# Packed q/k projections, 1024-column score tiles and one static order for a gated attention and token-MLP kernel on one core

## The chip, the cores and the metric

The kernel runs on one core of one Trainium2 chip. The metric is the device time of one launch in microseconds (us). A kernel's time is the median of its runs; the page and the trace of a kernel come from one profiled run of it.

The engines are named as the profile names them: PE is TensorE (PEld its weight loads, which overlap with matmuls: 216.0 us of them beside 362.7 us of matmuls in a span of 402.6), DVE is VectorE, ACT is ScalarE, POOL is GpSimd, SP is SyncE, which here only starts transfers. Each engine works through its own list of instructions in order, and waits on semaphores for the others.

## The reference, cut to what matters

The input x is 2048 x 640. A is attention with a compressive memory: 32 heads of 20 columns, four segments of 512 rows. Within a segment it is causal softmax attention; from segment 1 on, a linear-attention read of a memory M that sums up earlier segments is mixed in. B normalises x by row and runs an MLP over the token axis. A gate per row mixes A and B.

```python
phi = lambda t: jnp.where(t > 0, t + 1.0, jnp.exp(t))
for s in range(N):                                  # N = 4 segments of L = 512
    qs, ks, vs = q[:, :, s], k[:, :, s], v[:, :, s]
    p = softmax(einsum('bhqd,bhkd->bhqk', qs, ks) * scale + mask)
    a_dot = einsum('bhqk,bhkd->bhqd', p, vs)
    a_mem = (phi(qs) @ M) / (phi(qs) @ z + 1e-06)
    o = g * a_mem + (1.0 - g) * a_dot
    M = M + phi(ks)^T vs ;  z = z + sum(phi(ks))
a = o @ wo                                          # [...]
h = layernorm(x)                                    # over 640 columns
u = gelu(einsum('bsd,sf->bdf', h, w1) + b1)         # 2048 tokens -> 1536
y = einsum('bdf,fs->bds', u, w2) + b2               # 1536 -> 2048 tokens
return gate * a + (1 - gate) * y^T                  # gate = sigmoid(x . gate_w)
```

## The kernel before

The parts that the change touches. A head takes 32 partitions (20 used), so a group of four heads fills 128 and there are 8 groups. The weights of q and k are copied into a zero-padded layout, and every segment needs 8 projections of q and 8 of k, each of 5 matmuls of 512 columns: 320 in all.

```python
# LayerNorm: statistics on DVE, scaling on ACT (3 of 4 tiles) and DVE (1 of 4)
if t % 4 != 3:
    nc.scalar.activation(out=hs[:, t, :], in_=xs[:, t, :], func=ACT.Identity, scale=..., bias=...)
else:
    nc.vector.tensor_scalar(out=hs[:, t, :], in0=xs[:, t, :], scalar1=mv[:, t, 0:1],
                            scalar2=rstd[:, t:t + 1], op0=ALU.subtract, op1=ALU.mult)
# [...] the whole first MLP matmul (w1, gelu) runs here, before any attention
nc.vector.tensor_copy(out=wq_pad[:]...[:, :, :, 1:1 + DH], in_=wq_st[:]...)   # likewise wk_pad

def phi(out_view, x_view, e_view):                  # DVE, ACT, DVE
    nc.vector.tensor_scalar_min(out=e_view, in0=x_view, scalar1=0.0)
    nc.scalar.activation(out=e_view, in_=e_view, func=ACT.Exp)
    nc.vector.scalar_tensor_tensor(out=out_view, in0=x_view, scalar=0.0, in1=e_view, op0=ALU.max, op1=ALU.add)

def st_exp(s, g):                                   # scores, two heads at a time
    for jt in range(TPS):
        Nq = L - jt * P                             # 512, 384, 256, 128 columns
        for hp in range(2):
            psB = pS("psB")
            for rr in range(2):
                nc.tensor.matmul(psB[:, rr, 0:Nq], lhsT=kA[32*r:32*r+32, ...], rhs=qA[32*r:32*r+32, ...],
                                 tile_position=(32 * r, 0))
            nc.scalar.activation(out=pt[...], in_=psB[:, :, 0:Nq], func=ACT.Exp, scale=SCALE)
        nc.gpsimd.affine_select(out=pt[:, :, 0:P], ...)     # causal mask of the diagonal block
# [...]
for s in range(NSEG):                               # the main loop; a scheduler interleaves
    for g in range(G):
        st_exp(s, g); pv_post(*prev)                # scores of this group, PV of the last one
        nat_v(s + 1, g); pg_q(s + 1, g); pg_k(s + 1, g); phi_kT(s + 1, g)   # next segment
        tail_y(...); tail_a(...); tail_b(...)       # second MLP matmul, output projection
```

## Time and profile before

The time before is 403.88 us (median of 3 runs, 403.81 to 411.12; a run more than 1.5% above the fastest, as 411.12 is, counts as slow). The head of the profile page gives busy time by engine, and the span in 40 equal slices with the busy share in tenths (PEclk is the clock that the TensorE throttle granted, in tenths of full speed).

```profile
PE 362.7 (90%) x3705; PEld 216.0 (54%) x3732; DVE 238.6 (59%) x556; ACT 235.0 (58%) x374; POOL 107.2 (27%) x162
PE   3559999959999999998999999999999999999976
POOL 8300000040132223434231323222222233343420
PEclk9759999998999999998999999999999999999998
```

PE is the engine that bounds this kernel: 362.7 of 402.6 us busy, at nine tenths or more in nearly every slice. The next table shows stretches of the span. Its columns are the stretch, its length, then busy us and instructions of PE, PEld, DVE, ACT and POOL, then granted clock, DMA share and GB/s.

```profile
0.00:27.00 27.00, 11.39 (x91) 8.85 (x92) 19.50 (x71) 19.36 (x32) 12.09 (x27) 0.80 0.97 281
27.00:80.00 53.00, 53.00 (x397) 37.84 (x395) 1.30 (x8) 22.35 (x36) 0.08 (x1) 0.97 0.43 118
58.00:104.00 46.00, 41.60 (x332) 25.45 (x333) 16.99 (x32) 14.09 (x24) 6.00 (x5) 0.96 0.16 39
104.00:140.00 36.00, 35.13 (x331) 20.85 (x333) 28.03 (x62) 16.86 (x28) 9.85 (x11) 1.00 0.01 2
88.00:390.00 302.00, 283.84 (x3084) 160.39 (x3110) 206.89 (x458) 192.35 (x305) 90.36 (x132) 0.99 0.08 24
```

From 27 to 80 us PE is busy without one gap, with the first MLP matmul (375 of the 397 instructions; the others are 20 tiny ones of the gate and the flag). From 88 to 390 us it is busy for 283.84 of 302 us, and no other engine is busy for more than 207. Three PE waits (total us, times, longest):

```profile
PE pg_352 L209 <- DVE cmask L270: 6.1, 1, 6.1
PE ptk_1013 L349 <- DVE phikT_990 L316: 2.6, 1, 2.6
PE psB_2444 L444 <- ACT PT_2429 L447: 1.2, 1, 1.2
```

The first lies in start-up (18.5 to 24.5 us): three tiny transposes that compute a flag (see below) wait for what DVE has reduced for them; the profile names cmask, which DVE finished just after it. The second is the longest after start-up. The third is the longest of the waits of a scores tile for the exponential that has its buffer; there are 28 of over 0.15 us, 8.4 us in all. One more number matters for what follows: DVE's own time for the LayerNorm scaling of one 128 x 640 tile, and for one 512-column step of phi (shortest, median and longest in ns, then first and last start).

```profile
L193 DVE TENSOR_SCALAR hs<-xs,mv,rstd x4: 441/443/444, 17.7 to 25.3; 128x640 bf16<-128x640 bf16 x4
L314 DVE TENSOR_SCALAR e_k_1033<-kA_969 x1: 282/282/282, 95.7 to 95.7; 128x512 bf16<-128x512 bf16 x1
```

### The profile page before, as it was taken

The page shows a single profiled execution, that of the slowest core. Times are in us where ns is not written, and L with a number is a line of the kernel's source. Part 1 is how long each engine was busy: PE and PEld are TensorE (multiplying, and loading weights), DVE is VectorE, ACT ScalarE, POOL GpSimd, SP SyncE. Part 2 cuts the span into 40 slices and gives each one's busy share as a digit, 9 for nine tenths or more (in the row PEclk, how much of TensorE's full clock was granted, in tenths as well). Part 3 has the DMA queues.
Part 4 walks back from the last instruction along what each step waited for, and adds up shares of the span by engine and source line. Part 5 has one row for each costly group of instructions (what it writes and reads, how often), then busy time and mean ns, then how long its engine had stood idle before and what let it go on. Part 6 is the DMA issues. An engine that isn't in the chain of part 4 may idle for free.

```text
span 402.6 us, 8992 instructions
## 1 busy us (share of the span) xinstructions
PE 362.7 (90%) x3705; PEld 216.0 (54%) x3732; DVE 238.6 (59%) x556; ACT 235.0 (58%) x374; POOL 107.2 (27%) x162
## 2 busy tenths in 40 slices
PE   3559999959999999998999999999999999999976
PEld 3437777734465555455555455555555554555544
DVE  5850000076886867766777778785766666444444
ACT  2999311233415677965565766655555767788740
POOL 8300000040132223434231323222222233343420
PEclk9759999998999999998999999999999999999998
DMA  6994454000000020020002000200020021000002
GB/s 224 330 314 119 126 154 108 2 0 2 0 2 2 2 79 2 2 80 2 0 18 81 18 2 19 78 18 2 20 80 18 10 74 31 18 2 18 18 21 72
DMA packets 32101, 21.78 MB, mean 54 GB/s; under 512 B 820, under 2 KB 32052, under 8 KB 32052
## 3 DMA queue, kind: packets, MB, share of 16 engines
q1 hardware_dynamic: 31842, 21.11, 18.0%
q8 instruction: 31, 0.51, 0.5%
q14 instruction: 18, 0.15, 0.1%
q10 hardware_dynamic: 210, 0.02, 0.0%
HBM read 18.50 MB, written 2.62 MB: 52 GB/s over the span
## 4 chain that ended last, share of the span: by engine, by line
PE 77%; ACT 12%; DVE 5%; issue 2%; DMA 2%; ACTq 0%; POOL 0%; DVEq 0%; POOLq 0%
DMA beta_bf<-in_A_beta_dram 2%; ACT xT L164 1%; PE pu_369 L234 1%; PE pu_370 L234 1%; DVE qA_968 L320 1%; DVE stats L182 1%; PE pu_772 L234 1%; PE pu_736 L234 1%; PE pu_700 L234 1%; PE pu_664 L234 1%; PE pu_628 L234 1%; PE pu_592 L234 1%; PE pu_554 L234 1%; PE pu_518 L234 1%; PE pu_480 L234 1%
## 5 line engine op out<-in xcount | busy, mean ns | idle before, releaser
L255 DVE TENSOR_SCALAR gt<-gt 128x16 f32<-128x16 f32 x1 | 2.1, 2073 | 40.6 <-ACT gt L254 40.6
L401 PEld LDWEIGHTS <-wk_pad 128*128 128x128 bf16 x160 | 14.8, 99 | 15.5 <-issue 1.4
L374 PEld LDWEIGHTS <-wq_pad 128*128 128x128 bf16 x160 | 12.4, 97 | 11.2 <-issue 2.9
L307 POOL MEMSET vs_970<- 128x128 bf16 x1 | 0.7, 664 | 66.6 <-PE pu_772 L234 66.6
L330 PEld LDWEIGHTS <-xT 128*128 128x128 bf16 x160 | 13.0, 97 | 7.1 <-issue 1.5
L182 DVE BATCH_NORM_STATS2 stats<-xs 128x6 f32<-128x320 bf16 x32 | 13.4, 460 | 4.0 <-DMA xs<-in_A_x_dram 4.0
L444 PEld LDWEIGHTS <-kA_969 32*128 32x128 bf16 x128 | 6.0, 90 | 17.5 <-issue 16.6
L444 PEld LDWEIGHTS <-kA_2515 32*128 32x128 bf16 x128 | 6.1, 90 | 16.4 <-issue 14.9
L444 PEld LDWEIGHTS <-kA_1310 32*128 32x128 bf16 x128 | 5.9, 91 | 15.8 <-issue 14.4
L444 PEld LDWEIGHTS <-kA_3832 32*128 32x128 bf16 x128 | 6.0, 91 | 12.5 <-issue 10.2
L190 ACT ACTIVATE hs<-xs,nmr,rstd 128x640 bf16<-128x640 bf16 x12 | 10.0, 924 | 0.0
L163 PEld LDWEIGHTS <-xs 128*128 128x128 bf16 x80 | 7.3, 126 | 4.5 <-issue 3.8
L234 PEld LDWEIGHTS <-w1c_126 128*128 128x128 bf16 x64 | 7.3, 114 | 3.9
L211 DVE TENSOR_REDUCE gred<-pg_352 1x1 f32<-1x128 f32 x1 | 0.3, 279 | 14.3 <-PE pg_352 L209 14.3
L234 PEld LDWEIGHTS <-w1c_515 128*128 128x128 bf16 x64 | 6.3, 98 | 2.4
L234 PEld LDWEIGHTS <-w1c_132 128*128 128x128 bf16 x64 | 6.3, 98 | 2.4
L234 PEld LDWEIGHTS <-w1c_441 128*128 128x128 bf16 x64 | 6.3, 98 | 2.4
L234 PEld LDWEIGHTS <-w1c_589 128*128 128x128 bf16 x64 | 6.3, 98 | 2.4
L234 PEld LDWEIGHTS <-w1c_130 128*128 128x128 bf16 x64 | 6.3, 98 | 2.4
L209 PE MATMUL pg_352<-ident_f,gstat 128*1 128x128 f32 x3 | 0.9, 306 | 6.1 <-DVE cmask L270 6.1
L234 PE MATMUL pu_369<-hs,w1c_126 128*128 128x320 bf16 x16 | 6.3, 405 | 0.0
L234 PE MATMUL pu_370<-hs,w1c_126 128*128 128x320 bf16 x16 | 6.2, 398 | 0.0
(1883 smaller groups left out, 1389.7 us busy)
## 6 DMA issues: line engine op xcount, KB each, us to landing
xs<-in_A_x_dram SPq DMA_DIRECT2D x4, 640.0 KB, 7.6
w1c_126<-in_B_w_dram SPq DMA_DIRECT2D x1, 1024.0 KB
w1c_130<-in_B_w_dram SPq DMA_DIRECT2D x1, 1024.0 KB
w1c_132<-in_B_w_dram SPq DMA_DIRECT2D x1, 1024.0 KB, 13.1
w1c_441<-in_B_w_dram SPq DMA_DIRECT2D x1, 1024.0 KB, 5.5
w1c_515<-in_B_w_dram SPq DMA_DIRECT2D x1, 1024.0 KB, 5.9
w1c_589<-in_B_w_dram SPq DMA_DIRECT2D x1, 1024.0 KB, 6.2
wq_st<-in_A_wq_dram SPq DMA_DIRECT2D x1, 800.0 KB, 14.0
```

What stands on the lines that cost most here:

```text
L163: nc.tensor.transpose(pt[:, j, :], xs[:, t0 + j, c * P:(c + 1) * P], ident_bf[:])
L164: nc.scalar.copy(out=xT[:, c, t0 * P:(t0 + ST // XC) * P], in_=pt[:].rearrange("p a b -> p (a b)"))
L182: nc.vector.bn_stats(out=stats[:, t, c, :], in_=xs[:, t, c * HALF:(c + 1) * HALF])
L190: nc.scalar.activation(out=hs[:, t, :], in_=xs[:, t, :], func=ACT.Identity, scale=rstd[:, t:t + 1], bias=nmr[:, t:t + 1])
L209: nc.tensor.transpose(pg[:, c, :], gstat[:, c:c + 1], ident_f[:])
L234: nc.tensor.matmul(pu[hh][:, 0:HALF], lhsT=w1c[:, t, f2 * P:(f2 + 1) * P], rhs=hs[:, t, hh * HALF:(hh + 1) * HALF], start=(t == 0), stop=( ...
L255: nc.vector.tensor_scalar(out=gt[:], in0=gt[:], scalar1=0.5, scalar2=0.5, op0=ALU.mult, op1=ALU.add)
L320: nc.vector.tensor_copy(out=out_view, in_=ps_view)
L330: nc.tensor.matmul(pv[hh][:, 0:HALF], lhsT=xT[:, c, t * P:(t + 1) * P], rhs=wv_sb[:, c, hh * HALF:(hh + 1) * HALF], start=(c == 0), stop=( ...
L374: nc.tensor.matmul(pq[:, 0:L], lhsT=wq_pad[:, c, g * P:(g + 1) * P], rhs=xT[:, c, s * L:(s + 1) * L], start=(c == 0), stop=(c == DC - 1))
L401: nc.tensor.matmul(pk2[:, 0:L], lhsT=wk_pad[:, c, g * P:(g + 1) * P], rhs=xT[:, c, s * L:(s + 1) * L], start=(c == 0), stop=(c == DC - 1))
L444: nc.tensor.matmul(psB[:, rr, 0:Nq], lhsT=kA[32 * r:32 * r + 32, g, jt * P:(jt + 1) * P], rhs=qA[32 * r:32 * r + 32, g, jt * P:L], start=T ...
```

## The change

The intent is to take TensorE work away and to fill every hole between scores with other work.

- q and k are projected without padding: 5 chunks of 128 of the 640 columns instead of 8 padded groups, so 200 matmuls of 512 columns instead of 320. In a packed chunk the first 20 rows of each 32 belong to group c, the other 12 carry a piece of groups 5, 6 or 7, which transfers on SP move to their own place.
- Scores go to tiles of 2 x 512 columns that join (g, 3) with (g, 1), and (g, 2) with (g + 1, 2). One visit (a run of scores matmuls between other work on PE) does all four heads: 80 visits instead of 224, and 160 exponentials of 1024 columns.
- LayerNorm scaling, and the add and the min of phi, go to GpSimd. So do two smaller steps that DVE did before: the sum of the two parts of attention and the scaling of M (39 operations). Statistics stay on DVE.
- Everything else on PE (projections, first and second MLP, memory update and read, tail) is a list of items, and a planner written in the kernel takes the next instructions from that list between two scores tiles. The order of each engine is then fixed as written.

```diff
-        nc.vector.tensor_copy(out=wq_pad[:].rearrange(...)[:, :, :, 1:1 + DH], in_=wq_st[:]...)
+    PIECES = [(0, 0, 12, 5, 0), (1, 0, 8, 5, 12), (1, 8, 4, 6, 0), (2, 0, 12, 6, 4),
+              (3, 0, 4, 6, 16), (3, 4, 8, 7, 0), (4, 0, 12, 7, 8)]
+        def ln_apply(ci):                      # [...]
+            nc.gpsimd.tensor_tensor(out=rstd[:, tsl], in0=rstd[:, tsl], in1=mhalf[:], op=ALU.pow)
+            for t in range(tsl.start, tsl.stop):
+                nc.gpsimd.tensor_scalar(out=xs[:, t, :], in0=xs[:, t, :], scalar1=mv[:, t, 0:1],
+                                        scalar2=rstd[:, t:t + 1], op0=ALU.subtract, op1=ALU.mult)
         def phi(out_view, x_view):
-            nc.vector.tensor_scalar_min(out=e_view, in0=x_view, scalar1=0.0)
-            nc.scalar.activation(out=e_view, in_=e_view, func=ACT.Exp)
-            nc.vector.scalar_tensor_tensor(out=out_view, in0=x_view, scalar=0.0, in1=e_view, ...)
+            nc.gpsimd.tensor_scalar(out=out_view, in0=x_view, scalar1=1.0, scalar2=None, op0=ALU.add)
+            nc.scalar.activation(out=e[:], in_=x_view, func=ACT.Exp)
+            # placed 0.8 and 2.2 us of PE work later:
+            nc.gpsimd.tensor_scalar_min(out=e[:], in0=e[:], scalar1=1.0)
+            nc.vector.tensor_tensor(out=out_view, in0=out_view, in1=e[:], op=ALU.max)
+        def mem_update(s, c):                  # transposes, copy, and at once the matmuls that read it
+            for j in range(TPS):
+                nc.tensor.transpose(ptk[:, j, :], pk_[:, j * P:(j + 1) * P], ident_bf[:])
+            nc.vector.tensor_copy(out=nat[:], in_=ptk[:])
+            # [...] matmuls: lhsT=nat[:, j, :]
+        def scores(s, parts):                  # all four heads, up to 2 x 512 columns each
+            tl = [pS("psB"), pS("psB")]
+            for (g, jt) in parts:
+                for r in range(HG):
+                    nc.tensor.matmul(tl[r // 2][:, r % 2, o:o + n], ..., tile_position=(32 * r, 0))
+            return [exp_mask(x, ps_off) for x in tl]
+        # [...] the list of items, in order
+        for t in range(8): add(("ln", t), ...)       # LayerNorm statistics
+        for ci in range(1, 4): add(("xT", ci), ...)  # transposes of x
+        for t in range(8, 16): add(("ln", t), ...)
+        for ci in range(4): call(("lnA", ci), ln_apply, ci)
+        call("flag", flag)
+        # qkv of segment 1; first MLP (merged with qkv of 2); second MLP, tail, qkv of 3
+        for (s, g) in pairs:
+            q0 = scores(s, [(g, 0)]);  filln();  post(*prev)
+            q13 = scores(s, [(g, 3), (g, 1)]);  filln()
+            q2 = scores(s, [(g, 2), (g + 1, 2)]);  filln()
+            # [...] two more visits for g + 1
```

The flag is a number that says whether scores could overflow without a row maximum. Before, it chose between two main parts; now the fast one always runs, and a slow one after it only if the flag says so. With this input it never does.

## The prediction

> What bounds it now. TensorE. The table of stretches gives PE 362.7 of 402.6 us busy: 0 to 27 us is start-up (PE 11.4 busy, loads, transposes, LayerNorm), 27 to 80 is the first MLP matmul alone (PE full, ACT 22 of 53, DVE 1.3), 88 to 390 is attention with everything else (PE 283.8 of 302, ACT 192, DVE 207). So what counts is PE stream time, the start, and whether PE is fed.
>
> PE stream time, from start-to-start distances in the timeline: a 512-column matmul takes 0.216 us (TensorE: Matmul & The Clock Gate, Part 1, states 215.7 ns; the trace agrees), 320 columns 0.136, a 128-column transpose about 0.056, a 21-column PV matmul 0.0255. A visit of scores between full-array matmuls displaces 0.42 us (all four 512s), 0.365 (a 384 pair), 0.31 (256), 0.26 (128), 0.2 of it not streaming. The TensorEngine Tiling page, Key Properties, says that a mode switch drains the array; those gaps agree. One head group: about 2.3 us in 7 visits.
>
> Removed on PE (estimates from these):
> - q/k projections 320 to 200 matmuls: 120 x 0.216 = 26 us.
> - Scores: 224 visits become 80 visits of all four heads, 512 columns each, about 0.45 us: 73 to 36 us, 37 saved.
> - Gate matmuls (80): 2 us. phi(k) transposes 96 to 60: 2 us; memory update and read grow by about 2 us.
> Sum of PE stream time: about 347 to 284 us.
>
> Moved. The MLP no longer runs ahead of attention, so ACT's exponentials spread over the whole run. The first quarter of x lands at 5.0 us (DVE's wait) and weights follow; first scores should start near 15 us instead of 87.
>
> Added. ACT: 160 exponentials of 1024 at 0.92 us spacing (147 us), 30 for phi, k, v and y evictions, 12 gelu of 640 columns, four gelu batches with two table loads (1.28 us each) per batch: about 225 us. GpSimd gets phi's add and min, LayerNorm, masks, packing: perhaps 200 us. Each scores visit needs both score buffers back, hence both previous exponentials. In about 3.4 us of PE work per visit ACT normally needs 1.9 to 2.9, so it keeps up; PE will wait in three places: the two weight norms (2 x 2.9 us) ahead of the first exponentials (about 5 us lost), four gelu batches (about 5 us of ACT each, about 3 lost each, 12 together), and the phi-heavy stretch of segments 0 and 1 (about 5 us).
>
> Sum: start 21 us of which 3 is useful PE work; 281 us streaming; 17 us ACT waits other than start; cold clock 2 us; tail and last output 6. Total about 327 us, 19% below.
>
> What would show it: PE busy share at least 90% from 25 us to the end; scores line with 80 visits and about half its former displaced time; projection matmuls 200; PE waits for score buffers concentrated after gelu batches and at 15 to 25 us; ACT 220 to 240 us busy; exponentials beginning before 25 us.
>
> What would make it wrong: the order is static, so PE may stall on evictions queued behind 2 us of exponentials on ACT (only four general PSUM buffers), or on slow GpSimd (masks before PV, LayerNorm before the MLP, packing before the first projection): each slot of 80 losing 0.3 us adds 24 us. If GpSimd's ops take over 1.2 us rather than 0.6, it becomes the bound in segments 0 and 1. If stalls are fully absorbed, 312 us.
>
> I predict 327 us, 8 in 10 between 311 and 346; faster by over 2% 0.985, within 2% 0.01, slower 0.005.

## The result, and the profile after

The changed kernel takes 441.74 us (median of 4 runs, 438.34 to 442.92) against 404.62 us of the kernel before beside it. The ratio is 1.088, with a 95% interval of 1.080 to 1.097: 9% slower, where I had predicted 19% faster. Ratios are over the fast runs alone, so not quite the ratio of the medians that are quoted. Results were right in all runs.

The page of the changed kernel, the same lines as before:

```profile
PE 323.0 (74%) x3553; PEld 204.9 (47%) x3568; DVE 166.1 (38%) x440; ACT 237.5 (54%) x300; POOL 261.1 (60%) x336
PE   3878743903732699799778677889979799898975
POOL 2697879999999232332898863424687433343420
PEclk9969865855985579999996979989989999999998
```

PE has 40 us less to do, and yet the span is 34 us longer: PE is busy for 74% of it. In the seven slices in a row where the POOL row stands at 9 (65 to 142 us) the PE row reads 3, 9, 0, 3, 7, 3 and 2, and PEclk falls to 5 in four of them. Two of the stretches shown before and the one after them, with the same columns:

```profile
58.00:104.00 46.00, 17.24 (x143) 10.47 (x141) 21.16 (x70) 11.97 (x20) 45.19 (x26) 0.62 0.01 3
104.00:140.00 36.00, 16.86 (x169) 8.82 (x172) 13.11 (x25) 14.35 (x20) 35.72 (x35) 0.74 0.06 12
140.00:420.00 280.00, 240.72 (x2834) 157.95 (x2845) 101.99 (x273) 177.48 (x217) 139.50 (x196) 0.93 0.21 56
```

In 58 to 104 us GpSimd is busy for 45.19 of 46 us, and PE for 17.24. In 104 to 140 us GpSimd is busy for 35.72 of 36 us, and PE for 16.86. Those two stretches alone hold 48 us of idle PE (82 less 34.1). The longest PE waits:

```profile
PE pacc_1092 L535 <- POOL PT_923 L518: 17.8, 1, 17.8
PE pg_886 L257 <- DVE gstat L254: 8.8, 1, 8.8
PE pm_208_1363 L396 <- DVE phiq_912 L299: 8.3, 2, 5.6
PE psB_1336 L497 <- ACT PT_1248 L508: 4.1, 1, 4.1
```

The 17.8 us can be followed. The timeline of GpSimd and then of PE (start, us, what, and in brackets the idle time before it and what ended it), with the end of the LayerNorm block:

```profile
59.52 9.96 POOL L213 TENSOR_SCALAR xs<-xs,mv,rstd 128x640 bf16<-128x640 bf16 x4
...
93.67 9.95 POOL L213 TENSOR_SCALAR xs<-xs,mv,rstd 128x640 bf16<-128x640 bf16 x4
103.56 0.66 POOL L285 MEMSET vs_909<- 128x128 bf16 x1
103.83 0.62 POOL L518 TENSOR_SCALAR_AFFINE_SELECT PT_923<-PT_923 128x256 bf16<-128x256 bf16 x1
...
106.79 1.51 POOL L292 TENSOR_SCALAR phiq_912<-qk_908 128x512 bf16<-128x512 bf16 x1
108.27 1.49 POOL L296 TENSOR_SCALAR e_1069<-e_1069 128x512 bf16<-128x512 bf16 x1
```

```profile
85.89 0.81 PE L309 MATMUL pq_1088<-xT,wq_p 128*128 128x512 bf16 x3
104.51 0.23 PE L535 MATMUL pacc_1092<-vs_195,PT_923 128*128 128x21 bf16 x2 [17.81 <-POOL PT_923 L518]
```

And the exponential whose output that mask works on, from ACT's timeline:

```profile
74.96 1.02 ACT L508 ACTIVATE PT_923<-psB_917 128x1024 bf16<-128x1024 f32 x1 [10.24 <-PE psB_918 L497]
```

The exponential was done at 75.98 us. Its mask started at 103.83, 27.9 us later, because GpSimd, without a gap, still had ten of the 16 LayerNorm scalings of 2.5 us each to do, with the small steps between them. The Trainium skill says in "Perfetto Trace Analysis", section "Tensor Engine Instruction (MATMUL, LD_WEIGHTS)", that ACT, DVE and GpSimd are strict first-in, first-out; this trace agrees. PE's next instruction in its static order was the PV matmul (softmax weights times v) that needs that mask. PE stood from 86.7 to 104.5 us, though projections of segment 1, which need nothing of that mask, were still to be done. Once the block is over, the add and min of phi follow at 1.46 us from start to start and keep GpSimd full to 140 us.

A table of my own splits each profiled span in three. "Stream" is PE's busy time as if all of it had run at full clock (busy time less half of what fell into stretches that the clock records give as half speed). "Half clock" is that half. "Idle" is the rest of the span.

```
             span    stream   half clock   idle     (us)
before       402.6   353.4      9.3        39.9
after        436.5   293.6     29.4       113.5
difference   +33.9   -59.8    +20.1       +73.6
```

So the TensorE work that the change was to remove was removed: 60 us. Against it stand 74 us more of waiting and 20 us more of half clock. The Trainium skill, "TensorE: Matmul & The Clock Gate", Part 1, says that the throttle gives half clock after an idle window of about 3.4 us and full clock after a busy one. The records agree on the window: the clock changes on a grid of 3.41 us, with 24.7 us at half clock before and 108.5 after. They do not agree that PE must stand for a whole window. In the kernel before, the clock fell at 183.33 us, and in the 3.41 us up to there PE was busy for 1.61 us and stood for at most 0.91 us at a time (the columns are those of the stretches above):

```profile
179.92:183.33 3.41, 1.61 (x19) 0.82 (x19) 3.09 (x8) 2.84 (x5) 0.84 (x2) 1.00 0.00 0
```

In the traces of all 14 kernels together the clock fell 115 times; PE had been busy for 0 to 72% of the 3.41 us before, and had stood for all of it in four cases only. So many short waits cost clock as well as a long one.

The idle time of 113.5 us is 5.3 before the first PE instruction, 5.2 after the last one, and 103.0 between; by what ended it:

```
PE idle between instructions, after (103.0 us in all; before: 29.5)
19.4 us in 15 waits   exponentials (ACT) before the next scores tile
18.8 us in  5 waits   masks (GpSimd) before PV
12.1 us in 15 waits   transposed phi(k) copied (DVE) before the memory update
10.7 us in  4 waits   phi(q) (DVE, behind GpSimd) before the memory read
 8.8 us in  1 wait    LayerNorm statistics (DVE) before the flag's transposes
 7.4 us in 10 waits   attention output copied (DVE) before the output projection
25.8 us               all others
```

### The profile page after: what moved, and what is told of

The parts are those of the page before. It is cut to its first block, busy times and chain, and to the rows that moved or that the text cites. A ratio compares the mean times of both kernels' runs of the same rounds, so it can differ in the third digit from the quotient of the medians.

```text
span 436.5 us, 8697 instructions
## 1 busy us (share of the span) xinstructions
PE 323.0 (74%) x3553; PEld 204.9 (47%) x3568; DVE 166.1 (38%) x440; ACT 237.5 (54%) x300; POOL 261.1 (60%) x336
## 5 line engine op out<-in xcount | busy, mean ns | idle before, releaser
L213 POOL TENSOR_SCALAR xs<-xs,mv,rstd 128x640 bf16<-128x640 bf16 x16 | 39.8, 2501 | 0.4
L482 PEld LDWEIGHTS <-late 128*128 128x128 bf16 x160 | 15.3, 103 | 16.8 <-DVE late L472 10.0
L336 PEld LDWEIGHTS <-xT 128*128 128x128 bf16 x160 | 16.6, 108 | 11.8 <-issue 2.4
L309 PEld LDWEIGHTS <-wk_p 128*128 128x128 bf16 x100 | 10.1, 104 | 14.7 <-issue 5.3
L309 PEld LDWEIGHTS <-wq_p 128*128 128x128 bf16 x100 | 9.6, 104 | 13.5 <-issue 7.0
L535 PE MATMUL pacc_1092<-vs_195,PT_923 128*128 128x21 bf16 x8 | 1.1, 182 | 17.8 <-POOL PT_923 L518 17.8
L292 POOL TENSOR_SCALAR phiq_1979<-qk_1975 128x512 bf16<-128x512 bf16 x5 | 7.5, 1493 | 5.4 <-DVE qk_1975 L313 5.4
L497 PEld LDWEIGHTS <-qk_908 20*128 20x128 bf16 x128 | 3.1, 92 | 15.4 <-issue 15.2
L497 PEld LDWEIGHTS <-qk_194 20*128 20x128 bf16 x128 | 2.9, 96 | 15.6 <-issue 13.6
L299 DVE TENSOR_TENSOR phiq_912<-phiq_912,e_1069 128x512 bf16<-128x512 bf16 x1 | 0.8, 821 | 23.5 <-POOL e_1069 L296 23.5
L435 ACT ACTIVATE uT<-upre,b1t 128x640 bf16<-128x640 f32 x12 | 9.2, 819 | 0.7 <-DVE upre L428 0.7
L425 PEld LDWEIGHTS <-w1c_2260 128*128 128x128 bf16 x64 | 7.0, 116 | 5.4 <-issue 1.6
L535 PEld LDWEIGHTS <-PT_923 128*128 128x128 bf16 x8 | 0.7, 107 | 18.3 <-POOL PT_923 L518 18.3
L425 PEld LDWEIGHTS <-w1c_1943 128*128 128x128 bf16 x64 | 5.9, 98 | 6.3 <-issue 3.7
L396 PEld LDWEIGHTS <-phiq_912 128*128 128x128 bf16 x48 | 3.5, 140 | 10.6 <-DVE phiq_912 L299 8.6
L292 POOL TENSOR_SCALAR phiq_3406<-qk_3402 128x512 bf16<-128x512 bf16 x5 | 7.5, 1494 | 0.9 <-DVE qk_3402 L313 0.8
L425 PEld LDWEIGHTS <-w1c_125 128*128 128x128 bf16 x64 | 6.2, 102 | 3.5 <-issue 1.1
L425 PEld LDWEIGHTS <-w1c_2581 128*128 128x128 bf16 x64 | 5.8, 98 | 4.2 <-issue 2.4
L292 POOL TENSOR_SCALAR phiq_912<-qk_908 128x512 bf16<-128x512 bf16 x5 | 7.5, 1492 | 0.3 <-DVE qk_908 L313 0.2
```

Source lines behind the costliest of these rows:

```text
L213: nc.gpsimd.tensor_scalar(out=xs[:, t, :], in0=xs[:, t, :], scalar1=mv[:, t, 0:1], scalar2=rstd[:, t:t + 1], op0=ALU.subtract, op1=ALU.mult)
L292: nc.gpsimd.tensor_scalar(out=out_view, in0=x_view, scalar1=1.0, scalar2=None, op0=ALU.add)
L309: nc.tensor.matmul(pq[:], lhsT=w[:, k, c, :], rhs=xT[:, k, s * L:(s + 1) * L], start=(k == 0), stop=(k == DC - 1))
L336: nc.tensor.matmul(pv[:, 0:n], lhsT=xT[:, c, t * P:(t + 1) * P], rhs=wv_sb[:, c, hh * HALF:hh * HALF + n], start=(c == 0), stop=(c == DC - 1))
L396: nc.tensor.matmul(pm[g // 5][:, g % 5, :], lhsT=phiq[:, c, it * P:(it + 1) * P], rhs=m[:, COFF[c] + CG[c].index(g), :], start=(i == 0), s ...
L425: nc.tensor.matmul(pu[:, 0:HALF], lhsT=w[:, t, (ft % 2) * P:(ft % 2 + 1) * P], rhs=xs[:, t, hh * HALF:(hh + 1) * HALF], start=(t == 0), st ...
```

## The experiments

All times are medians of four runs (six for the last). Ratios are against runs of the kernel before. The experiments were run in four calls on four chips, and the changed kernel in one more; between kernels of two calls the ratios are the safer comparison.

### Is it GpSimd's durations? Three single moves

My theory was that GpSimd, as a queue in order with operations 2.5 times longer than I had assumed, holds up masks and phi, and through them PE. The rival was that the static order itself stalls PE on many short producer-to-consumer waits on any engine, so that a faster engine would gain little.

```diff
 # e1_ln_dve: LayerNorm scaling on DVE (16 operations)
-                nc.gpsimd.tensor_scalar(out=xs[:, t, :], in0=xs[:, t, :], scalar1=mv[:, t, 0:1],
+                nc.vector.tensor_scalar(out=xs[:, t, :], in0=xs[:, t, :], scalar1=mv[:, t, 0:1],
 # e2_phi_dve: the add and the min of phi on DVE (60 operations)
-            nc.gpsimd.tensor_scalar(out=out_view, in0=x_view, scalar1=1.0, scalar2=None, op0=ALU.add)
+            nc.vector.tensor_scalar(out=out_view, in0=x_view, scalar1=1.0, scalar2=None, op0=ALU.add)
-                nc.gpsimd.tensor_scalar_min(out=e[:], in0=e[:], scalar1=1.0)
+                nc.vector.tensor_scalar_min(out=e[:], in0=e[:], scalar1=1.0)
 # e3_both_dve: both edits
```

> Only the 16 LayerNorm scalings of 640 columns move from GpSimd (2.49 us each in the changed kernel) to VectorE (0.44 us each for the same form in the kernel before). Theory G (GpSimd's slow elementwise work, in one in-order queue ahead of the causal masks, starves PE): the 45 us block at 58 to 103 us shrinks to under 15 us, the 17.8 us wait of PV for the mask goes, and the time falls from about 441 to about 405 us; the phi-bound stretch of segment 1 stays. Theory S (the static order and the score visits that need both buffers are the cause, GpSimd only shows it): 430 us or more, the wait moving to another producer.

> Only phi's add and min (60 operations of 512 columns, 1.49 us each on GpSimd) move to VectorE (0.29 us for such a min in the kernel before). Theory G: GpSimd busy 261 to about 171 us, the PE-starved stretch 104 to 140 us shrinks to about 10 us, the LayerNorm block stays; about 405 us. Theory S: 430 us or more.

> Both moves together. Theory G: GpSimd about 130 us busy, granted clock back above 0.94, PE busy share above 85%, 345 to 360 us, that is faster than the kernel before by over 10%. Theory S: above 400 us.

| kernel | us | ratio to before [95%] |
|---|---|---|
| e1_ln_dve | 428.76 | 1.055 [1.048, 1.063] |
| e2_phi_dve | 413.75 | 1.020 [1.011, 1.029], unclear |
| e3_both_dve | 396.95 | 0.977 [0.970, 0.983], unclear |

The direction was right and the sizes were not. Against the changed kernel's 441.74, one move gains 13 us, the other 28 (30 without the one of its runs that counts as slow, 416.83), both together 45. In e1 the mask wait of 17.8 us is no longer among the longest, but the run lost some of it elsewhere. Its longest PE waits now are:

```profile
PE psB L497 <- ACT PT L508: 18.7, 15, 3.4
PE pg L257 <- DVE gstat L254: 14.7, 1, 14.7
PE pdm L374 <- DVE knat L363: 12.1, 15, 2.1
```

In e3, where GpSimd is busy for 134.2 of 394.1 us only, the waits are:

```profile
PE pg L257 <- DVE gstat L254: 14.7, 1, 14.7
PE pdm L374 <- DVE knat L363: 13.4, 15, 2.1
PE psB L497 <- ACT PT L508: 12.2, 11, 3.2
```

My sum for e3 had been 345 to 360 us. So GpSimd is one cause, of 45 us, and not the only one. What e3 has left is the rival's: 79.9 us of idle PE with no engine near full.

### Was the saved TensorE time worth anything in this order?

If PE's stream bounds the changed kernel, putting back the 120 projection matmuls (as redundant ones, whose result is overwritten) costs 120 x 0.216 = 26 us. If waits bound it, most of that vanishes in waits.

```diff
 # e4_after_padcost
             pq = p1([P, 512], name="p" + which)
+            for _ in range(3):
+                nc.tensor.matmul(pq[:], lhsT=w[:, 0, c, :], rhs=xT[:, 0, s * L:(s + 1) * L],
+                                 start=True, stop=True)
```

> The changed kernel with 3 redundant 512-column matmuls ahead of each of its 40 projections, so that it streams 320 of them again as the kernel before does (about 26 us of PE stream at full clock). If PE stream bounded the changed kernel the time would rise by about 26 us; under theory G many of the projections lie in starved or cold stretches, so that the rise differs: under 15 us if they fall into waits.

It took 447.75 us, 6 us more than the changed kernel (the two ratios, 1.101 and 1.088, differ by 1.2%, and their intervals overlap, so that even the 6 us are not clear of noise). It was run at another time. The stream grew by 23.5 us (to 317.1) and the idle time fell by 16.1. In this order, at least about three quarters of the padding that was saved had bought nothing.

### A single wait moved: the flag

The longest wait of e3 is the flag's. DVE has the LayerNorm statistics of 16 tiles in two batches, and behind them the 16 scalings; the flag's transposes stand in PE's order right behind, and need a reduction that is last on DVE. From e3's timeline of DVE:

```profile
68.91 0.83 DVE L205 BATCH_NORM_STATS2 stats<-xs 128x6 f32<-128x320 bf16 x2
69.78 0.21 DVE L206 BATCH_NORM_AGGREGATE mv<-stats 128x2 f32<-128x12 f32 x1
69.90 6.17 DVE L213 TENSOR_SCALAR xs<-xs,mv,rstd 128x640 bf16<-128x640 bf16 x16
```

Nothing needs the flag before the end of the kernel. If that one wait is the cost, moving it behind the first MLP gains up to 14.7 us. If DVE's backlog is the cost, the next PE instruction that needs something of DVE will wait instead.

```diff
 # e6_flag_late (on e3)
-        call("flag", flag)
         add(("gate", 0), 0, gate, 0)
 # [...] first MLP
         merge(b1_items[8:], qkv_items(2))
+        call("flag", flag)
```

> On e3_both_dve (397 us; there PE waits 14.7 us for the safety flag's three transposes, which need all LayerNorm statistics): the flag alone moves to after the first MLP matmul. Theory D (the 16 statistics tiles, 16.5 us in one block on VectorE, hold up every eviction behind them; the flag is only where it shows): PE meets the block again at the evictions of v and of x and gains little, 388 to 397 us. Theory F (the flag's place itself): the whole 14.7 us and part of the cold clock go, 375 to 382 us. Theory A (ACT and the score buffers bound it): no gain, 395 us or more.

It took 393.96 us, ratio 0.978 [0.970, 0.986]: 3 us less than e3 by the medians, and no difference by the ratios. The flag's wait is gone, and a new one is there, for the copy of a v tile that stands in DVE's queue behind the same block:

```profile
PE pv L336 <- DVE gl L344: 6.9, 1, 6.9
```

So the backlog was there to be met again, as Theory D had said. But that is half of the account. In the profiled runs idle time did fall, by 8.9 us (79.9 to 71.0), and the half-clock loss rose by 8.7 (18.5 to 27.1). How much of that rise is chance is not settled: over all their runs the granted clocks of e3 (0.901 to 0.914) and e6 (0.897 to 0.910) overlap.

### The backlog spread, then producers an item ahead

The next edit keeps e6's work and spreads DVE's: the statistics of one tile per item of segment 0, and the scalings one by one between segment 1's projections.

```diff
 # e7_stats_spread (on e6), core of it
         for c in range(1, DC):
             add_proj(0, c, "q")
+            next_ln()                      # statistics of one tile of x
             add_proj(0, c, "k")
+            next_ln()
 # [...]
-        for t in range(8):
-            add(("ln", t), 0, ...)
-        for ci in range(4):
-            call(("lnA", ci), ln_apply, ci)
-        for f in qkv_items(1):
-            f()
+        merge(qkv_items(1), [lambda t=t: call(("lnA", t), ln_scale, t) for t in range(ST)])
```

> On e6: one statistics tile after each item of segment 0's projections, and the 16 scalings between the items of segment 1, so that VectorE has no block of over 2 us. Theory D: PE idle between 55 and 80 us goes, half clock time shrinks by 20 us or more, 365 to 378 us. Theory F: little beyond e6. Theory A: no gain, the waits become waits of scores for exponentials (over 25 us instead of 12).

The second edit keeps e7's order but puts the producer of a value one item ahead of its user: the transposes of phi(k) for chunk c + 1 go ahead of the update matmuls of chunk c, the transposes of the attention output between the two halves of the second MLP, and the two sums of squares of the weights (2.9 us each on ACT) behind segment 0's projections.

```diff
 # e8_split (on e7), core of it
-            return [lambda: add(("mu", s, c), ..., mem_update, s, c)]
+            r = [lambda: add(("mt", s, c), 4 * 56, mem_transpose, s, c)]
+            if c >= 1:
+                r.append(lambda: add(("mu", s, c - 1), ..., mem_add, s, c - 1))
+            # [...] the last one after its own transposes
-        weight_norms()
+        call("norms", weight_norms)        # moved behind segment 0's items
-                r.append(lambda: add(("ta", t), 5 * 56, tail_a, t))
+                r.insert(1, lambda: add(("ta", t), 5 * 56, tail_a, t))
```

> On e7: in PE's order something else stands between a producer and its use: the memory update's transposes come an item ahead of its matmuls (13.4 us of waits for their copies in e3), the transposed attention tile an item ahead of its matmul (5.3 us), and the two weight norms (5.8 us on ACT) come after segment 0's projections instead of ahead of the first exponentials. Theory O (the static order's waits are a sum of such short ones, each paid in full): 15 to 25 us less than e7, 345 to 358 us. Theory A: under 8 us gained, waits of scores for exponentials rise.

| kernel | us | ratio to before [95%] | stream | half clock | idle |
|---|---|---|---|---|---|
| e6_flag_late | 393.96 | 0.978 [0.970, 0.986], unclear | 294.2 | 27.1 | 71.0 |
| e7_stats_spread | 384.85 | 0.953 [0.947, 0.959] | 294.1 | 20.5 | 68.0 |
| e8_split | 359.25 | 0.891 [0.886, 0.897] | 292.9 | 18.4 | 45.9 |

e7 gained 9 us and missed what Theory D had (365 to 378 us, and 20 us less time at half clock; that time fell by 16 us, from 77 to 61). One reason is in the next lines: the waits of the memory update rose from 13.0 us in e6 to 18.5, as the statistics now stand between the copies that it needs.

e7's memory update and its wait, first from its list of PE waits, then from its timeline of PE:

```profile
PE pdm L375 <- DVE knat L364: 18.5, 15, 2.7
```

```profile
49.00 0.39 PE L361 MATMUL ptk<-ident_bf,phik 128*128 128x128 bf16 x4
51.49 0.33 PE L375 MATMUL pdm<-vs,knat 128*128 128x84 bf16 x4 [2.11 <-DVE knat L364]
```

Four transposes take 0.39 us, the copy on DVE about 0.42 once its turn comes, and PE stands for 2.1 us because its order has nothing between them. In this case DVE began the copy 1.7 us after the transposes had ended, since one step of phi and two of the spread statistics were ahead of it in its queue. In e8:

```profile
PE psB L509 <- ACT PT L520: 7.9, 7, 2.8
PE pdm L386 <- DVE knat L368: 4.3, 4, 2.6
```

The update's wait falls by 14.2 us, the exponentials' from 12.9 to 7.9, and idle time by 22.1 in all, with the same stream. The edit bundles three moves, so these waits are all that attributes its 26 us; runs of the single moves were not made.

### In the better order, do the change's savings count, and do GpSimd's durations?

Three kernels built on e8 undo one thing each. The padding first: if PE now bounds the kernel, 120 redundant matmuls cost about 26 us; if waits still do, far less. The edit is e4's.

> e8 with the 120 redundant projection matmuls of e4. If e8 is bound by PE stream the rise is close to the full 120 x 0.216 = 26 us (20 to 27), against the 6 us that the same matmuls added to the changed kernel (447.8 beside 441.7). If e8 is bound by ACT or by waits: under 12 us.

It took 370.66 us, 11.4 more than e8 (ratio 0.920 [0.913, 0.927]). The stream grew by 22.6 us, idle time fell by 7.2, and the half-clock loss by 5.4. Half of the added work still vanished in waits, but about half of the saving now reaches the time; in the order of the changed kernel it was a quarter.

Second, the scores visits. Each four-head visit is cut in two, with other PE work between, which gives 160 visits instead of 80 and the same number of columns.

```diff
 # e10_visits_split (on e8), core of it
+            for h in range(2):
+                for (g, jt) in parts:
+                    for r in range(2 * h, 2 * h + 2):
+                        nc.tensor.matmul(tl[h][:, r % 2, o:o + n], ..., tile_position=(32 * r, 0))
+                if h == 0:
+                    fill(130)              # one matmul of another item in between
```

> e8 with every score visit cut in two: two heads, one full-array matmul (or the next piece of other work), then the other two heads; 80 visits become 160. By the trace of the kernel before a two-head visit of 512 columns displaces about 0.42 us, as much as the four-head one, so about 80 x 0.42 = 34 us of PE stream more. If e8 is near its PE bound: 15 to 30 us slower (e9's 26 us of matmuls added 11, the rest fell into idle time). If the visits cost nothing because ACT paces them: under 5 us.

It took 386.98 us, 27.7 more than e8 (24 by the ratios; ratio 0.950 [0.942, 0.958]). It was run at another time. The stream grew by 30.7 us, 0.38 per added visit. One of the cut visits in its timeline of PE:

```profile
246.47 0.39 PE L514 MATMUL psB<-qk 20*128 20x128 bf16 x4
246.79 0.31 PE L469 MATMUL py<-uT,w2c 128*128 128x320 bf16 x1
247.03 0.39 PE L514 MATMUL psB<-qk 20*128 20x128 bf16 x4
```

The lone full-array matmul between the halves takes 0.24 us from its start to the next one's, where such a matmul takes 0.136 in a row of its kind. The Trainium skill, "TensorEngine Tiling (Array Packing)", Key Properties, says that a change of tiling mode drains the array; visits that cost 0.38 us each without adding a column agree with it. So joining the visits was worth its trouble. The 0.38 us is the price of one more visit with a lone matmul beside it and can't be carried over to the 144 visits that the change removed, for which the prediction had counted 37 us: at 0.38 each they would be 55 us, and with 23 for the padding that is more than the 60 us by which the stream fell. Of those 60 us, the padding leaves 37.

Third, the operations of e1 and e2 back on GpSimd, in the order of e8. If GpSimd's durations are the cause whatever the order, this costs what e3 had gained, 45 us; if the bad order was what made them cost, much less.

> e8 with phi's add and min and the LayerNorm scaling put back on GpSimd, the order kept. In the changed kernel's own order moving them to VectorE saved 45 us. Theory G (GpSimd's durations are the cause, whatever the order): 35 us or more above e8, 395 or more. Theory OG (mostly the order: one block of LayerNorm ahead of the masks): under 20 us above e8.

It took 415.04 us, 56 more than e8 (52 by the ratios; ratio 1.021 [1.013, 1.028]). Only the engine of 76 operations differs between those two kernels, and the chain that the profile follows back from the end of the run now goes through GpSimd for 35% of the span, in e8 for 1%. The lines by engine, of e8 and then of e12:

```profile
PE 65%; DVE 15%; ACT 11%; issue 4%; DMA 3%; POOL 1%; SPq 0%; DVEq 0%; POOLq 0%; ACTq 0%
```

```profile
PE 43%; POOL 35%; DVE 10%; ACT 6%; DMA 3%; issue 2%; SPq 0%; POOLq 0%; DVEq 0%; ACTq 0%
```

The duration of one operation in e12, against DVE's 0.28 and 0.44 us for the same forms (shown with the kernel before):

```profile
L214 POOL TENSOR_SCALAR xs<-xs,mv,rstd x16: 2496/2508/2533, 69.0 to 146.5; 128x640 bf16<-128x640 bf16 x16
L293 POOL TENSOR_SCALAR phik<-qk x15: 1488/1493/1657, 15.2 to 239.0; 128x512 bf16<-128x512 bf16 x15
```

Which operation PE waits for is not the same as in the changed kernel: here its waits for masks come to 0.3 us. From 80 to 140 us GpSimd is busy for 59.8 of 60 us. DVE waits 89 us in all for phi's min, and what PE waits for comes late from there (8.0 us for one phi(q)), or it is a scaled row of the first MLP (8.1 us). So it is the full queue that costs, and not the masks as such. DVE's own step of phi, the max, also became slower: the same 30 instructions take 24.5 us in e12 and 12.3 in e8, most of them 0.6 to 1.0 us while GpSimd works and 0.37 to 0.43 where it does not. No run took that apart from the rest. Nor was the order of e8 fitted to GpSimd's durations, so a better order for them may exist.

Together with e3, e8 and the changed kernel this is a table of two by two, in which only the order differs along a row and only the engine of the 76 operations down a column:

```
                          changed order    order of e8
76 operations on GpSimd   441.74           415.04  (e12)
76 operations on DVE      396.95  (e3)     359.25  (e8)
```

The engine alone is worth 45 us, the order alone 27, and both 82. Each is worth more once the other is mended: 56 and 38. (By the ratios 45, 27 and 80, and then 52 and 34.)

### How far does the order go?

Two more steps on e8. The first interleaves the transposes of x with the projections of segment 0, and puts the memory reads and updates of segment 1 between halves of the first MLP. The second cuts the two sums of squares on ACT in ten pieces, since a wait of 4.9 us behind them was left.

```diff
 # e11_interleave (on e8), core of it
-        for ci in range(1, 4):
-            add(("xT", ci), 20 * 56, x_transposes, ci)
+        merge(rest, [lambda ci=ci, c=c: add(("xT", ci, c), 4 * 56, x_transpose, ci, c)
+                     for ci in range(1, 4) for c in range(DC)])
-        merge(b1_items[:8], [])
+        merge(b1_items[:8], q1[16:])
 # e13_norm_pieces (on e11), core of it
-            nc.scalar.activation(out=wjunk[:], in_=wq_st[:], func=ACT.Square, accum_out=gstat[:, 1:2])
+            nc.scalar.activation(out=wj[0][:, c, :], in_=(wq_st, wk_st)[i][:, c, :], func=ACT.Square,
+                                 accum_out=gpart[:, i, c:c + 1])
```

> e8 with the short, dependent pieces spread: segment 0's remaining transposes of x one column block at a time between its last projections and memory updates; segment 1's memory reads and updates between the first eight MLP halves instead of in one run (80 to 105 us of e8, where PE is 56% busy and its clock halved). Theory O: 8 to 14 us less than e8, 345 to 351 us, time at half clock below 25 us. Theory A (ACT paces): under 3 us.

> e11 with the two weight norms (2.87 us each in one block on ACT at 54 to 60 us, behind which the gate, an eviction of v and PE wait 4.9 us) cut into ten pieces of 640 columns between the items of segment 1. Theory O (each block in an in-order queue is paid by whoever stands behind it): 3 to 7 us less than e11's 352, 345 to 349 us. If the wait only moves (the same ACT time is due before segment 1's evictions anyway): under 2 us.

e11 took 352.22 us (ratio 0.863 [0.855, 0.871]), 7.0 less than e8 by the medians, a little less gain than I had expected, and 11 by the ratios. Its time at half clock is 38 us, and I had expected less than 25. e13 took 351.11 us (six runs, ratio 0.865 [0.860, 0.869]): no gain, as in the case that the wait only moves. In the profile of e13 the wait of 4.9 us is gone, and the idle time of that run is lower by 5.6 us, but its half-clock loss is higher by 2.3 and its stream by 1.4, and the ratios of the two are the same. e11 is the best version by its ratio, 13.7% faster than the kernel before and 20% faster than the changed one.

The accounts of all the kernels side by side, one profiled run each (columns as in the table of the result):

```
                    span    stream   half clock   idle    POOL busy
before              402.6   353.4      9.3        39.9     107.2
after               436.5   293.6     29.4       113.5     261.1
e1_ln_dve           426.2   294.2     35.3        96.6     222.7
e2_phi_dve          408.6   291.2     25.6        91.9     173.1
e3_both_dve         394.1   295.8     18.5        79.9     134.2
e4_after_padcost    445.7   317.1     31.3        97.4     261.1
e6_flag_late        392.3   294.2     27.1        71.0     134.3
e7_stats_spread     382.6   294.1     20.5        68.0     134.1
e8_split            357.1   292.9     18.4        45.9     133.8
e9_split_padcost    367.1   315.5     13.0        38.7     134.0
e10_visits_split    387.4   323.6     18.4        45.4     134.0
e11_interleave      351.0   292.0     16.2        42.8     133.6
e12_split_pool      413.0   289.9     33.7        89.4     259.9
e13_norm_pieces     349.1   293.4     18.5        37.2     133.6
```

The stream column hardly moves except where matmuls or visits were added on purpose. All the rest is waiting, and the half clock that mostly goes with it. How much of the half-clock loss is a mere consequence of the waits was not isolated: it falls with idle time from after to e3 and from e6 to e8, but not run by run (e1 and e6 have less idle time than the kernels they were built on, and more half clock).

## Why the prediction was wrong

Point by point, as the prediction put it.

- "Sum of PE stream time: about 347 to 284 us." Right in what it saves: the records give 353.4 to 293.6, 60 us where 63 were predicted, though both ends are 6 to 10 us higher. Of its terms, the 120 matmuls measured 22.6 to 23.5 us (26 predicted); the term of the visits (37) was not measured by itself, and fits what is left of the 60.
- "ACT 220 to 240 us busy" and "exponentials beginning before 25 us": right, 237.5 us and 22.84 us. The wait for the two weight norms ahead of them was there as well.
- "GpSimd gets phi's add and min, LayerNorm, masks, packing: perhaps 200 us." This is the first term that failed. It measured 261.1 us. The 60 phi operations take 1.49 us each and the 16 scalings 2.50 us; my "0.6 us" for an operation was right for the masks only (86 us for 160 in e3). Worse than the sum is where it sits: all of the LayerNorm block and most of segment 1's phi lie between 58 and 140 us, ahead of masks that PE needs. The prediction had named the threshold ("over 1.2 us rather than 0.6, it becomes the bound in segments 0 and 1") and put the chance of slower at 0.005, although the kernel before had not one GpSimd operation of this kind to read a duration from. The runs size this at 45 us in the changed order (e3) and 56 us in a better one (e12). It is the largest single cause that they show.
- "PE will wait in three places." This is the second term that failed. The prediction had 18 us of start, 17 us of ACT waits and 6 us of tail, 41 us of idle PE in all; it measured 113.5. Part of the missing terms is GpSimd's, counted above: 18.8 us for masks and 10.7 for phi(q). The rest are waits of a static order in which a consumer follows its producer at once, among them 12.1 us for the memory update, 7.4 for the output projection and 8.8 (14.7 in e3) behind DVE's statistics. In e3, with GpSimd out of the way, 79.9 us of idle remained; e6 to e11 took 37 us of that away by nothing but reordering. The prediction had named stalls of the static order as what would make it wrong, and left them out of its sum.
- "Cold clock 2 us." The third, 29.4 us. An order with gaps pays twice, since PE runs at half speed after stretches with enough of them; the kernel before lost 9.3 us so.
- "PE busy share at least 90% from 25 us to the end": wrong, 75% from 25 us on (310.25 of 411.5 us); by this test, which the prediction itself gave, its step on waits is the one that fell.
- "If stalls are fully absorbed, 312 us." Not reached by any order I ran. In e11 (span 351.0 us) PE is idle for 42.8 us, which is what the prediction had for idle time (41); the 24 us by which it lies above 327 are 14 us more of half clock (16.2 against 2), 8 of stream (292.0 against 284) and these 2.

The plan of the change was thus right and its bill was not. The kernel before spent 53 us on the first MLP with PE full, after LayerNorm had been done by ACT and DVE in the first 27 us. The changed kernel gave up that dependence-free block (no run put it back, so what it was worth is not shown), and moved 76 elementwise operations to the engine that is five times slower at them and that also gates PV.

## What to carry to other kernels

Before moving elementwise work to an idle engine, get one measured duration of that very form there, and look at what else its queue gates: 27.9 us of lateness for a mask came from operations that nobody was waiting for yet. When PE's order is written by hand, put every producer that hops over another engine at least one item ahead of its consumer, and judge by idle time and half clock together, since in e6, without the longest wait, 8.9 us less of idle time stood beside 8.7 us more of half clock. A saving of PE time counts only as far as PE is the bound: the same 120 matmuls were worth 6 us in the changed order and 11 us in the better one, against 26 by their duration.

## What the Trainium skill lacked or had wrong

- "GPSIMD Engine Reference", section 4.1 (Engine selection), says that GpSimd is about 2 times slower than VectorE for operations of two inputs and that those of one input run roughly at line rate. For `tensor_scalar` on bf16 in SBUF, one input, these runs show 1.49 us against 0.28 for 128 x 512 (5 times), and 2.50 against 0.44 for 128 x 640 with two steps and per-partition scalars (5.7 times). The measurement decides. The page's tables are for fp32 and have no row for bf16 or for `tensor_scalar`.
- The same page has no figure for short operations: raising 128 x 4 numbers to a power took 1.04 us, a causal mask (`affine_select`) 0.41 us for 128 x 256 and 0.64 for 128 x 512 (e3).
- "Perfetto Trace Analysis", section "GPSIMD Engine Instruction", advises to time GpSimd by start-to-start spacing rather than by the reported duration. Here the two agree within 3%: 1.46 us of spacing for a reported 1.49, 2.49 for 2.50.
- "TensorEngine Tiling (Array Packing)", Key Properties, says that a switch of tiling mode drains the array, and gives no price. 80 more visits of scores, with the same columns, cost 30.7 us of PE time, 0.38 us a visit, including the break in the other item's row of matmuls.
- "TensorE: Matmul & The Clock Gate", Part 1, gives no share of busy time below which a window counts as idle. Here the clock fell after windows of 3.41 us in which PE was busy for up to 72%, and from full speed it fell after every window in which PE was busy for less than 43%.
